# Linear attention and SwiGLU on one core: loads of a batch held until the features of the batch ahead are turned, q loaded first, first batch in fewer loads, first two weight blocks alone

## The chip, the core and the metric

The kernel runs on one core of a Trainium2 chip. A core has five engines with an instruction stream each: TensorE (PE; its weight loads are shown apart as PEld), VectorE (DVE), ScalarE (ACT), GpSimd (POOL) and SyncE (SP). Sixteen DMA engines move data between device memory (HBM) and on-chip memory (SBUF); here POOL's queue issues the loads that cast float32 to bfloat16, and SP's queue issues the first batch's float32 loads, the transposing DMAs and the output stores. TensorE writes to PSUM, eight banks of 128 x 512 float32. The metric is the device time of one execution in microseconds (us); less is better.

## The reference

q, k and v have 8 batches, 8 heads, 576 positions and 64 elements a head. The attention is linear: a feature map of 128 elements for q and for k, and no softmax. Its output, 4608 tokens of 512, goes through a SwiGLU block with 1536 hidden elements.

```python
def _attn_ref(q, k, v):
    theta = np.pi / 2.0 * pos / S
    def phi(x, c, s):
        r = np.maximum(x, 0.0)
        return np.concatenate([r * c, r * s], axis=-1)
    q_p, k_p = phi(q, cos_w, sin_w), phi(k, cos_w, sin_w)
    kv = np.einsum('bhsf,bhsd->bhfd', k_p, v)
    z = np.sum(k_p, axis=2)
    num = np.einsum('bhsf,bhfd->bhsd', q_p, kv)
    den = np.einsum('bhsf,bhf->bhs', q_p, z)[..., None] + 1e-06
    return num / den

def _moe_ref(x, w_gate, w_val, w_out):
    g = x @ w_gate
    silu = g * (1.0 / (1.0 + np.exp(-g)))
    return silu * (x @ w_val) @ w_out
```

## The kernel before

**Tiles and groups.** Positions are cut into 9 slices of 64 per batch, 72 in all. Two slices make a tile of 128 tokens (36 tiles, t), four tiles make a group of 512 tokens (9 groups, tg). Batch b begins at slice 9b, so a tile can span two batches: tile 13 holds the last slice of batch 2 and the first of batch 3. Tiles 9 to 12 are of batch 2 alone.

**The feed-forward of a group.** `ffn_fc` (line 492) computes one block fc of 128 hidden elements: four products with w_gate and four with w_val (L480), a Silu on ScalarE (L488) and a product on DVE (L490). There are 12 blocks. Then `ffn_out` (L499) does the output product of each of the four tiles, 12 products each (L507), copies it from PSUM (L514) and stores it with two DMAs on SP (L517).

**Attention of a batch, from batch 2 on.** Everything is written once per batch into slots of the feed-forward's schedule:

- `load(b, nm)` (L94) loads q, k or v of a batch on POOL's queue into one of three buffers per tensor (`raw`, bufs=3).
- `phi_q(b, g)` (L224), for each of four pairs of heads g: relu on ScalarE (L213), product with the table of cosines and sines on DVE (L230), into `r_q`.
- `relu_k` and `vmul` (L217, L233): relu of k on ScalarE (on DVE for batch 1), v times the table on DVE (L234), into `v2s` (two buffers).
- `qturn_dma(b, e)` (L250): the features of half of the heads are turned by a transposing DMA on SP's queue, from `r_q` to `phit[b][:, e]` (L253; `phit` has two buffers).
- `kv_mm(b, j)` (L267), 36 products each (L276), and `kv_out2` (L294), which copies the sums out.
- `a_tile2(t)` (L369): 8 products of the turned features with the sums (L380; 16 where the tile spans two batches), then the normalisation on DVE (L391, L393, L398). The first four wait for half e=0 of the features, the others for e=1.
- `x_turn(t)` (L447): the normalised tile is turned, by a transposing DMA on SP (L465) or, with fast, by TensorE and a copy on ScalarE (L462, L463).

Batches 0 and 1 take other paths. Batch 0's v, k and part of q are loaded as float32 on SP's queue (`load_first`, L114) into memory that w_out and the hidden activations use later. Its k is cast and clipped by `relu_first_k` (L221), and `kv_first` (L304) makes the sums in two halves.

**Slots.** `plan` maps a slot number to functions; `at(s, f)` adds one and `slot(s)` calls them, in the order in which they were added. Group tg has the slots 16 tg to 16 tg + 15: one after each of the 12 blocks, then one after each of the four output tiles. In the loop over b (L655), s0 = 16 (b - 1) is the first slot of the group ahead of the one in which the batch's middle tiles are computed, and p0 = s0 - 16. For b of 3 and more, before the change, the eight steps of k, v and q stand in slots p0 + 3 to p0 + 10 (one later for b = 3), the turning DMAs in p0 + 12 and p0 + 13, the kv products in s0 + 1 and s0 + 2. For b = 2 they stand in s0 to s0 + 3, s0 + 2, and s0 + 4 and s0 + 5.

**What sets the order.** The schedule is written by hand (`manual_schedule`): each engine runs its instructions in the order in which the program emits them, and waits only for data and for buffers. POOL has hardly anything but DMA issues after the start, so the slot in which a load is emitted fixes only its place in POOL's queue. At the start, POOL waits with the tiny copy into `hold` (L541) for v's second pair of heads; then it issues the weights in pairs of 128 columns (`load_w`, L199: w_gate, then w_val), with the loads of batch 0's remaining q and of batch 1 between them, then w_out and batch 2. PSUM banks are handed out by `take`, the one longest unused first.

**Lines the change touches.** 118 to 125 (first loads), 199 (`load_w`), 540 to 556 (POOL's first queue), 580 and 581 (first relus), 655 to 690 (slots of the batches, slots of the tiles, loads of batch 3).

Of the kernel before, what the change touches and what calls it, by code (L numbers as in the profile page):

```python
# [10 lines left out]
BF16 = mybir.dt.bfloat16  # L11
# [6 lines left out]
def kernel(  # L18
# [10 lines left out]
    nc = tc.nc  # L29
    B, H, S, D = q.shape  # L30
    P = 128
    G = H // 2
# [13 lines left out]
    consts = ctx.enter_context(tc.tile_pool(name="consts", bufs=1))  # L46
# [38 lines left out]
    def source(b, nm):  # L85
        t = {"q": q, "k": k, "v": v}[nm]
        return t[b].rearrange("(g e) (p c) d -> (e p) g (c d)", e=2, c=NC)

    def raw_of(b, nm):
        if (b, nm) not in raws:  # L90
            raws[b, nm] = raw.tile([P, G, NC, D], BF16, name=f"raw_{nm}")
        return raws[b, nm]

    def load(b, nm, parts=1):  # L94
        t, sv, n = raw_of(b, nm), source(b, nm), G // parts
        for i in range(parts):
            sl = slice(i * n, (i + 1) * n)
            nc.gpsimd.dma_start(out=t[:, sl].rearrange("p g c d -> p g (c d)"), in_=sv[:, sl])  # L98

    def load_slots(b, nm, lo, hi):  # L100
        nc.gpsimd.dma_start(out=raw_of(b, nm)[:, :, lo:hi].rearrange("p g c d -> p g (c d)"),
                            in_=source(b, nm)[:, :, lo * D:hi * D])
# [11 lines left out]
    def load_first(nm, gs, lo=0, hi=NC):  # L114
        nc.sync.dma_start(out=first[nm][:, gs, lo:hi].rearrange("p g c d -> p g (c d)"),
                          in_=source(0, nm)[:, gs, lo * D:hi * D])

    for gs in (slice(0, 1), slice(1, 2), slice(2, 4)):
        load_first("v", gs)
    load_first("k", slice(0, 1))  # L120
    load_first("k", slice(1, 2))
    load_first("q", slice(0, G), 0, 2)
    load_first("k", slice(2, 3))
    load_first("k", slice(3, 4))
    load_first("q", slice(0, G), 2, 4)
    NW = 8
    pos = consts.tile([P, NC], FP32)
# [17 lines left out]
    def idle_products(n, cols=P):  # L145
# [37 lines left out]
        out=tab.rearrange("p c e d -> p (c e) d"),  # L183
        in_=csk.rearrange("p c e -> p (c e)").to_broadcast([P, NC * 2, D]),
# [11 lines left out]
    wv_r = moe_w_val.rearrange("(c p) f -> p c f", p=P)  # L196
    wo_r = moe_w_out.rearrange("(c p) f -> p c f", p=P)

    def load_w(i):  # L199
        fs = slice(2 * i * P, (2 * i + 2) * P)  # L200
        nc.gpsimd.dma_start(out=wg_sb[:, :, fs], in_=wg_r[:, :, fs])  # L201
        nc.gpsimd.dma_start(out=wv_sb[:, :, fs], in_=wv_r[:, :, fs])

    def load_wo(i):
        cs = slice(4 * i, 4 * i + 4)
        nc.gpsimd.dma_start(out=wo_sb[:, cs], in_=wo_r[:, cs])
# [4 lines left out]
    def relu_op(eng, out, in_):  # L211
        if eng == "act":
            nc.scalar.activation(out=out, in_=in_, func=AF.Relu)  # L213
        else:
            nc.vector.tensor_single_scalar(out=out, in_=in_, scalar=0.0, op=ALU.max)

    def relu_k(b, lo, hi, eng):  # L217
        o = raw_of(b, "k")[:, lo:hi]
        relu_op(eng, o, o)

    def relu_first_k(g, eng, lo=0, hi=NC):  # L221
        relu_op(eng, raw_of(0, "k")[:, g, lo:hi], first["k"][:, g, lo:hi])

    def phi_q(b, g):  # L224

        if g == 0:
            st[b, "q"] = rel.tile([P, G, NC, 2, D], BF16, name="r_q")
        o = raws[b, "q"][:, g]
        relu_op("act", o, o)
        nc.vector.tensor_tensor(out=st[b, "q"][:, g], in0=o.unsqueeze(2).to_broadcast([P, NC, 2, D]),  # L230
                                in1=tab, op=ALU.mult)

    def vmul(b, g):  # L233
        nc.vector.tensor_tensor(  # L234
            out=v2s[b % 2][:, g, :, :, 0:D],
            in0=(first if b == 0 and g == 0 else {"v": raw_of(b, "v")})["v"][:, g].unsqueeze(2).to_broadcast([P, NC, 2, D]),
            in1=tab, op=ALU.mult,
        )
# [9 lines left out]
    phit = {}  # L248

    def qturn_dma(b, e):  # L250
        if e == 0:
            phit[b] = phip.tile([P, 2, G, NC, SH], BF16, name="phit")
        nc.sync.dma_start_transpose(  # L253
            out=phit[b][:, e].rearrange("p g c s -> p (g c) s"),
            in_=st[b, "q"][e * SH:(e + 1) * SH].rearrange("p g c w d -> p (g c w d)"),
        )
# [10 lines left out]
    def kv_mm(b, j):  # L267
        if j == 0:
            st[b, "kvps"] = take(2, ("kv", b))
        ps = st[b, "kvps"]  # L270
        for c in range(NC):
            for i in range(2):
                for e in range(2):
                    es = slice(e * SH, (e + 1) * SH)
                    g = 2 * j + i
                    nc.tensor.matmul(  # L276
                        out=ps[i * D:(i + 1) * D, e, j * 2 * D1:(j + 1) * 2 * D1],
                        lhsT=raws[b, "k"][es, g, c],
                        rhs=v2s[b % 2][es, g, c, :, 0:D1],
                        start=(c == 0), stop=(c == NC - 1),  # L280
                    )
# [12 lines left out]
    def kv_out2(b):  # L294

        ps = st[b, "kvps"][:, :, 0:4 * J * D1 // 2].rearrange("p e (j w x) -> p e j w x", j=J, w=2)
        for w, eng in enumerate((nc.scalar.copy, nc.vector.tensor_copy)):
            for i in range(2):
                eng(out=kv2s[b % 2][w * D:(w + 1) * D, :, :, i], in_=ps[i * D:(i + 1) * D, :, :, w])

    def kv_free(b):
        give_back(("kv", b))
# [26 lines left out]
    def cast_q(c, eng):  # L329
        o = qf[:, c % 2].rearrange("p j i d -> p (j i) d")  # L330
        (nc.scalar.copy if eng == "act" else nc.vector.tensor_copy)(out=o, in_=first["q"][:, :, c])
# [206 lines left out]
    for g in range(G):  # L538
        vmul(0, g)
    hold = consts.tile([P, 1], FP32)  # L540
    nc.gpsimd.tensor_copy(out=hold, in_=first["v"][:, 1, 0, 0:1])  # L541
    load_w(0)
    load_slots(0, "q", CUT[0], NC)
    for i in range(1, 4):
        load_w(i)
    load(1, "k")
    load_w(4)
    load_w(5)
    load(1, "v", 2)
    load_slots(1, "q", 0, CUT[1])  # L550
    load_wo(0)
    load_wo(1)
    load_slots(1, "q", CUT[1], NC)
    load_wo(2)
    for nm in ("k", "v", "q"):
        load(2, nm)

    OUT = GH // 2
    SLOTS = FC + OUT
    plan = {}  # L560

    def at(s, *fns):
        plan.setdefault(s, []).extend(fns)

    def slot(s):
        for f in plan.pop(s, ()):
            f()

    def a_(t, j):
        return lambda: (a_half(t, j), x_norm(t) if j else None)  # L570

    def turn(t, fast=False):
        return lambda: x_turn(t, fast)
# [4 lines left out]


    relu_first_k(0, "act")  # L580
    relu_first_k(1, "act")
    cast_q(0, "dve")
    cast_q(1, "dve")
    kv_first(0)
# [65 lines left out]
    for i, (piece, t) in enumerate(steps0):  # L650
        ffn_out(t, 4 * piece, 4 * piece + 4)
        slot(divmod(i, 4))


    for b in range(2, B):  # L655
        s0 = SLOTS * (b - 1)
        keng = "dve" if b == 2 else "act"
        steps = [lambda b=b, g=g: (relu_k(b, g, g + 1, keng), vmul(b, g)) for g in range(G)]
        steps += [lambda b=b, g=g: phi_q(b, g) for g in range(G)]
        if b == 2:  # L660
            steps = steps[G:] + steps[:G]
            fs, tq, tk = [s0 + i // 2 for i in range(8)], (s0 + 2, s0 + 2), (s0 + 4, s0 + 5)
        else:
            p0 = s0 - SLOTS
            fs = [p0 + 3 + i + (b == 3) for i in range(8)]
            tq, tk = (p0 + 12, p0 + 13), (s0 + 1, s0 + 2)
            if b > 3:
                for s, nm in ((p0 - 2, "k"), (p0, "v"), (p0 + 2, "q")):
                    at(s, lambda b=b, nm=nm: load(b, nm))
        for s, f in zip(fs, steps):  # L670
            at(s, f)
        for e in range(2):
            at(tq[e], lambda b=b, e=e: qturn_dma(b, e))
        for j in range(J):
            at(tk[j], lambda b=b, j=j: kv_mm(b, j))
        at(tk[-1], lambda b=b: kv_out2(b))
        at(tk[-1] + 1, lambda b=b: kv_free(b))
    for t in range(2 * OUT, NTG * OUT):
        tg, i = divmod(t, OUT)
        s = SLOTS * (tg - 1) + (4 if tg > 2 or i == 0 else 5) + 2 * i  # L680
        if t == 2 * OUT:
            at(s, a_(t, 0))
            at(s + 1, a_(t, 1), turn(t))
        elif tg == 2:
            at((10, 11, 12)[i - 1] + SLOTS, lambda t=t: a_tile2(t))
            at((12, 13, 14)[i - 1] + SLOTS, turn(t, True))
        else:
            at(s, lambda t=t: a_tile2(t), turn(t))
    for nm in ("k", "v", "q"):
        load(3, nm)  # L690
    for tg in range(1, NTG):
        s0 = SLOTS * tg
        for fc in range(FC):
# [39 lines left out]
```

## Time and profile before

| | us |
|---|---|
| runs | 352.4, 348.9, 351.09 (median 351.09) |
| the profiled execution | 351.02 |
| its span | 348.9 |
| TensorE busy | 324.5 (93%) |
| DVE busy | 179.3 (51%) |
| ScalarE busy | 134.9 (39%) |
| POOL busy | 31.6 (9%) |

The span runs from the first to the last instruction of the program; 2.1 us of the execution lie around it. Mean granted TensorE clock over the span: 0.974 of full speed.

How to read the lines. In the 40 slices a digit is the busy share of a slice in tenths, 9 is 90% or more. The timeline gives the start, the duration, the engine, the line, the operation and how many were merged, and in brackets how long the engine was idle just before and what ended that. In the chain of waits a row is the start, the length and what the chain went through; a DMA's row lasts from its issue to its landing. In groups of instructions the bar is followed by the busy time and the mean ns of one, then the idle time before them. A DMA issue is told with the median time from issue to landing. DMA-issuing instructions of SP are not counted as busy; the time shown for them is how long they hold SP's queue.

### The profile page before, as it was taken

The numbers are of one execution on the slowest core, as the hardware profiler recorded it, in microseconds if no ns is written. First come the engines' busy times: TensorE is split into PE (matmuls) and PEld (weight loads), VectorE is DVE, ScalarE is ACT, GpSimd is POOL, SyncE is SP. The second block draws the span as 40 slices with busy tenths as digits, with TensorE's granted clock in tenths as the row PEclk, the third lists the DMA queues.
The fourth block names the chain that finished last, engine by engine and source line by source line (L and its number), as shares of the span: only waits on it lengthen the run. The fifth ranks groups of instructions, "written<-read, shape, count | busy, mean of one in ns | idle before, by whom it ended". The sixth has DMA issues, their size and how long they took to land.

```text
span 348.9 us, 6209 instructions
## 1 busy us (share of the span) xinstructions
PE 324.5 (93%) x2484; PEld 165.6 (47%) x2484; DVE 179.3 (51%) x365; ACT 134.9 (39%) x253; POOL 31.6 (9%) x49
## 2 busy tenths in 40 slices
PE   8889999992079999999999999999999999999995
PEld 4577855440034444445445444544444444444443
DVE  6674766980072497149625952694256225603320
ACT  6544365972013464146414632562242123213321
POOL 7545320020000100020000000000000000000000
PEclk9999999998569999999999999999999999999999
DMA  7999999999926895789395129413931230231004
GB/s 226 238 200 201 203 208 233 233 160 134 134 38 114 147 190 75 128 138 195 62 152 107 31 49 154 86 30 72 152 72 39 57 81 15 41 81 45 2 22 98
DMA packets 69852, 40.51 MB, mean 116 GB/s; under 512 B 43584, under 2 KB 64320, under 8 KB 69824
## 3 DMA queue, kind: packets, MB, share of 16 engines
q1 hardware_dynamic: 49584, 22.55, 35.8%
q0 software_dynamic: 20080, 17.44, 32.4%
q8 instruction: 19, 0.31, 0.4%
q10 hardware_dynamic: 160, 0.13, 0.1%
q14 instruction: 9, 0.07, 0.1%
HBM read 37.75 MB, written 9.44 MB: 135 GB/s over the span
## 4 chain that ended last, share of the span: by engine, by line
PE 83%; DMA 14%; POOL 1%; issue 0%; ACT 0%; ACTq 0%; SPq 0%; DVE 0%; DVEq 0%
PE banks L480 50%; PE banks L507 26%; DMA phit<-r_q 6%; DMA wv_sb<-in_moe_w_val_dram 4%; DMA wg_sb<-in_moe_w_gate_dram 3%; PE banks L276 3%; PE banks L380 2%; DMA wo_sb<-in_v_dram 1%; PE banks L415 1%; PE banks L526 0%; PE banks L462 0%; PE banks L262 0%; POOL hold L541 0%; POOL wg_sb L201 0%; ACT ob L529 0%
## 5 line engine op out<-in xcount | busy, mean ns | idle before, releaser
L488 ACT ACTIVATE sg<-banks 128x512 bf16<-128x512 f32 (+2 forms) x124 | 67.2, 542 | 130.1 <-PE banks L480 122.1
L480 PE MATMUL banks<-xT,wv_sb 128*128 128x512 bf16 (+2 forms) x496 | 114.6, 354 | 1.4 <-DMA wv_sb<-in_moe_w_val_dram 1.4
L480 PE MATMUL banks<-xT,wg_sb 128*128 128x512 bf16 (+2 forms) x496 | 114.8, 354 | 0.1
L490 DVE TENSOR_TENSOR ht<-sg,banks 128x512 bf16<-128x512 bf16 (+2 forms) x124 | 76.4, 617 | 60.4 <-PE banks L480 51.3
L507 PE MATMUL banks<-wo_sb,ht 128*128 128x512 bf16 x420 | 94.3, 379 | 0.0
L480 PEld LDWEIGHTS <-wv_sb 128*128 128x128 bf16 x496 | 47.6, 98 | 48.6 <-DMA wv_sb<-in_moe_w_val_dram 1.8
L480 PEld LDWEIGHTS <-wg_sb 128*128 128x128 bf16 x496 | 44.8, 98 | 39.7 <-issue 0.6
L507 PEld LDWEIGHTS <-ht 128*128 128x128 bf16 x420 | 40.5, 98 | 46.7 <-issue 0.4
L514 DVE COPY ob<-banks 128x512 f32<-128x512 f32 x17 | 11.7, 691 | 64.7 <-PE banks L507 60.2
L514 ACT COPY ob<-banks 128x512 f32<-128x512 f32 x18 | 10.5, 586 | 58.4 <-PE banks L507 58.4
L380 PE MATMUL banks<-kv,phit 128*128 128x65 bf16 (+1 forms) x240 | 12.0, 198 | 16.6 <-DMA phit<-r_q 16.6
L230 DVE TENSOR_TENSOR r_q<-raw_q,tab 128x1152 bf16<-128x1152 bf16 x24 | 17.9, 751 | 18.7 <-DMA phit<-r_q 18.7
L234 DVE TENSOR_TENSOR v<-raw_v,tab 128x1152 bf16<-128x1152 bf16 x31 | 23.1, 753 | 2.2 <-ACT raw_v L537 2.2
L380 PEld LDWEIGHTS <-phit 128*128 128x128 bf16 (+1 forms) x240 | 10.7, 103 | 24.1 <-DMA phit<-r_q 17.3
L398 DVE TENSOR_TENSOR x<-banks,rec 128x512 bf16<-128x512 f32 (+1 forms) x32 | 21.5, 674 | 1.1
L213 ACT ACTIVATE raw_k<-raw_k 128x576 bf16<-128x576 bf16 x24 | 16.0, 675 | 0.0
L213 ACT ACTIVATE raw_q<-raw_q 128x576 bf16<-128x576 bf16 x24 | 16.0, 674 | 0.0
L98 POOL DMA_DIRECT2D raw_k<-in_k_dram x7 | 5.2, 742 | 98.3 <-issue 63.3
L276 PEld LDWEIGHTS <-raw_k 64*64 64x64 bf16 x504 | 7.8, 106 | 5.6 <-issue 4.7
L148 PE MATMUL banks<-zeros 128*128 128x64 bf16 (+1 forms) x64 | 9.4, 311 | 1.0 <-DVE zeros L143 1.0
L276 PE MATMUL banks<-v,raw_k 64*64 64x130 bf16 x504 | 10.2, 220 | 0.0
L463 ACT COPY xT<-banks 128x512 bf16<-128x512 bf16 x10 | 5.9, 588 | 3.9 <-PE banks L462 3.9
(81 smaller groups left out, 129.4 us busy)
## 6 DMA issues: line engine op xcount, KB each, us to landing
out_dram<-ob SPq DMA_DIRECT2D x70, 128.0 KB, 2.4
raw_k<-in_k_dram POOLq DMA_DIRECT2D x7, 576.0 KB, 16.5
raw_v<-in_v_dram POOLq DMA_DIRECT2D x6, 576.0 KB, 18.6
raw_q<-in_q_dram POOLq DMA_DIRECT2D x6, 576.0 KB, 20.8
wg_sb<-in_moe_w_gate_dram POOLq DMA_DIRECT2D x6, 256.0 KB, 12.2
wv_sb<-in_moe_w_val_dram POOLq DMA_DIRECT2D x6, 256.0 KB, 12.2
wo_sb<-in_moe_w_out_dram POOLq DMA_DIRECT2D x3, 512.0 KB, 13.1
ht<-in_k_dram SPq DMA_DIRECT2D x4, 288.0 KB, 6.6
```

Of the source, the lines that this page charges most:

```text
L148: nc.tensor.matmul(out=ps, lhsT=zeros, rhs=zeros[:, 0:cols].unsqueeze(1).to_broadcast([P, 4, cols]), start=True, stop=True)
L213: nc.scalar.activation(out=out, in_=in_, func=AF.Relu)
L230: nc.vector.tensor_tensor(out=st[b, "q"][:, g], in0=o.unsqueeze(2).to_broadcast([P, NC, 2, D]), in1=tab, op=ALU.mult)
L234: nc.vector.tensor_tensor(out=v2s[b % 2][:, g, :, :, 0:D], in0=(first if b == 0 and g == 0 else {"v": raw_of(b, "v")})["v"][:, g].unsqueez ...
L276: nc.tensor.matmul(out=ps[i * D:(i + 1) * D, e, j * 2 * D1:(j + 1) * 2 * D1], lhsT=raws[b, "k"][es, g, c], rhs=v2s[b % 2][es, g, c, :, 0:D ...
L380: nc.tensor.matmul(out=ps[ms, e, g * D1:(g + 1) * D1], lhsT=phit[b][:, e, g, c:c + n].rearrange("p c s -> p (c s)"), rhs=kv2s[b % 2][:, e, ...
L398: nc.vector.tensor_tensor(out=xv[:, :, ys], in0=num[:, :, ys, 0:D], in1=rv[:, :, ys].to_broadcast([P, 2, ys.stop - ys.start, D]), op=ALU.mult)
L480: nc.tensor.matmul(out=o, lhsT=w[:, kc, fs], rhs=xT[tg][:, ts, kc], start=(kc == 0), stop=(kc == KC - 1))
L488: nc.scalar.activation(out=sg[:, 0:n], in_=ps[0], func=AF.Silu)
L490: nc.vector.tensor_tensor(out=hts[tg % 2][:, fc, r:r + n], in0=sg[:, 0:n], in1=ps[1], op=ALU.mult)
L507: nc.tensor.matmul(out=o_ps[t], lhsT=hts[tg % 2][:, fc, r:r + P], rhs=wo_sb[:, fc], start=(fc == 0), stop=(fc == FC - 1))
L514: (nc.scalar.copy if t % 2 == 0 else nc.vector.tensor_copy)(out=ob, in_=ps)
```

## The change

Six edits:

1. The first batch: v in two loads of two pairs of heads, k in two, with q's two parts between and behind them; six DMAs on SP in place of nine.
2. `load_w(i, n)` loads n blocks of 128 columns from block i; the first two blocks are loaded alone, the other ten in pairs as before.
3. `relu_first_k(1)` runs on DVE in place of ScalarE.
4. Batch 2 is loaded in the order q, k, v (before: k, v, q).
5. The loads of batches 3 to 7 are emitted by `load_behind(b)`, in slot p0 + 3 for batch 3 and p0 + 1 for the others, q first. A POOL copy of two elements of `phit[b - 1]`, one of each half, stands ahead of them in POOL's queue.
6. Slots for b of 3 and more: the q steps come ahead of the k and v steps, all from p0 + 11 on; turning DMAs in p0 + 15 and p0 + 16; kv products in s0 + 4 and s0 + 5 as for batch 2. The tiles of group 3 and later move one slot back (4 + 2i becomes 5 + 2i). The rule for group 2 is written differently, and its tiles keep their slots.

```diff
-    for gs in (slice(0, 1), slice(1, 2), slice(2, 4)):
-        load_first("v", gs)
-    load_first("k", slice(0, 1))
-    load_first("k", slice(1, 2))
+    load_first("v", slice(0, 2))
+    load_first("v", slice(2, 4))
+    load_first("k", slice(0, 2))
     load_first("q", slice(0, G), 0, 2)
-    load_first("k", slice(2, 3))
-    load_first("k", slice(3, 4))
+    load_first("k", slice(2, 4))
     load_first("q", slice(0, G), 2, 4)
...
-    def load_w(i):
-        fs = slice(2 * i * P, (2 * i + 2) * P)
+    def load_w(i, n=2):
+
+        fs = slice(i * P, (i + n) * P)
...
-    load_w(0)
+    load_w(0, 1)
+    load_w(1, 1)
     load_slots(0, "q", CUT[0], NC)
-    for i in range(1, 4):
+    for i in (2, 4, 6):
         load_w(i)
     load(1, "k")
-    load_w(4)
-    load_w(5)
+    load_w(8)
+    load_w(10)
...
-    for nm in ("k", "v", "q"):
+    for nm in ("q", "k", "v"):
         load(2, nm)
...
-    relu_first_k(1, "act")
+    relu_first_k(1, "dve")
...
+    def load_behind(b):
+
+        nc.gpsimd.tensor_copy(out=hold2, in_=phit[b - 1][0:1, :, 0, 0, 0])
+        for nm in ("q", "k", "v"):
+            load(b, nm)
...
-        steps = [lambda b=b, g=g: (relu_k(b, g, g + 1, keng), vmul(b, g)) for g in range(G)]
-        steps += [lambda b=b, g=g: phi_q(b, g) for g in range(G)]
+        steps = [lambda b=b, g=g: phi_q(b, g) for g in range(G)]
+        steps += [lambda b=b, g=g: (relu_k(b, g, g + 1, keng), vmul(b, g)) for g in range(G)]
         if b == 2:
-            steps = steps[G:] + steps[:G]
-            fs, tq, tk = [s0 + i // 2 for i in range(8)], (s0 + 2, s0 + 2), (s0 + 4, s0 + 5)
+            fs, tq = [s0 + i // 2 for i in range(8)], (s0 + 2, s0 + 2)
         else:
             p0 = s0 - SLOTS
-            fs = [p0 + 3 + i + (b == 3) for i in range(8)]
-            tq, tk = (p0 + 12, p0 + 13), (s0 + 1, s0 + 2)
-            if b > 3:
-                for s, nm in ((p0 - 2, "k"), (p0, "v"), (p0 + 2, "q")):
-                    at(s, lambda b=b, nm=nm: load(b, nm))
+            fs, tq = [p0 + 11 + i for i in range(8)], (p0 + 15, p0 + 16)
+            at(p0 + 3 if b == 3 else p0 + 1, lambda b=b: load_behind(b))
+        tk = (s0 + 4, s0 + 5)
...
-        s = SLOTS * (tg - 1) + (4 if tg > 2 or i == 0 else 5) + 2 * i
+        s = SLOTS * (tg - 1) + (5 if tg > 2 else 4) + 2 * i
...
-    for nm in ("k", "v", "q"):
-        load(3, nm)
```

More of the change, by code (lines that the diff above doesn't have):

```diff
@@ L540 @@
     hold = consts.tile([P, 1], FP32)
+    hold2 = consts.tile([1, 2], BF16)
     nc.gpsimd.tensor_copy(out=hold, in_=first["v"][:, 1, 0, 0:1])
-    load_w(0)
+    load_w(0, 1)
+    load_w(1, 1)
     load_slots(0, "q", CUT[0], NC)
-    for i in range(1, 4):
+    for i in (2, 4, 6):
         load_w(i)
     load(1, "k")
-    load_w(4)
-    load_w(5)
+    load_w(8)
+    load_w(10)
     load(1, "v", 2)
```

## The prediction

> **What bounds the kernel now.** I read the page's 40 slices first, then the chain of waits, then the timeline around the gap. One slice is 348.9 / 40 = 8.72 us.
>
> ```profile
> PE   8889999992079999999999999999999999999995
> PEclk9999999998569999999999999999999999999999
> DMA  7999999999926895789395129413931230231004
> ```
>
> TensorE is full from slice 3 on except around slices 9 to 11 (a gap near 87 us), where its granted clock (PEclk, tenths) falls to a half; and the DMA engines are full from the start right up to that hole. After it they are seldom full. The chain of waits says what TensorE waited for, and shows undisturbed stretches of the same work further on:
>
> ```profile
> 69.41 1.73 PE banks L480 x8
> ...
> 76.21 21.52 DMA phit<-r_q
> ...
> 97.78 0.40 PE banks L380 x4
> 98.18 3.41 PE banks L480 x8
> ...
> 101.99 2.59 PE banks L507 x12
> ...
> 104.80 0.26 PE banks L380 x8
> ...
> 113.28 3.45 PE banks L480 x16
> ...
> 127.14 0.38 PE banks L380 x16
> ...
> 136.77 10.36 PE banks L507 x48
> ...
> 170.39 10.36 PE banks L507 x48
> ```
>
> Timeline, TensorE, with the idle time before each row in brackets:
>
> ```profile
> 79.72 1.03 PE L480 MATMUL banks<-xT,wv_sb 128*128 128x512 bf16 x4
> 88.55 0.40 PE L380 MATMUL banks<-kv,phit 128*128 128x65 bf16 x4 [7.80 <-DMA phit<-r_q]
> 97.78 0.40 PE L380 MATMUL banks<-kv,phit 128*128 128x65 bf16 x4 [8.83 <-DMA phit<-r_q]
> ```
>
> This is tile 9, the first that reads the turned q features of batch 2: it waits 7.80 us for the first half and 8.83 us for the second, 16.63 us in all. Why those two transposes were late (POOL's and SP's queues; then all twelve transposes: shortest, median and longest ns on SP's queue, and us to landing):
>
> ```profile
> 53.70 0.74 POOL L98 DMA_DIRECT2D raw_q<-in_q_dram  x1 [5.35 <-PE banks L262]
> 72.33 0.74 POOL L98 DMA_DIRECT2D raw_k<-in_k_dram  x1 [17.89 <-issue]
> 120.41 0.74 POOL L98 DMA_DIRECT2D raw_k<-in_k_dram  x1 [45.44 <-issue]
> 65.60 27.46 SPq L253 DMA_TRANSPOSE phit<-r_q  x2
> 105.23 1.80 SPq L517 DMA_DIRECT2D out_dram<-ob  x2
> 107.13 3.60 SPq L253 DMA_TRANSPOSE phit<-r_q  x1
> L253 SPq DMA_TRANSPOSE phit<-r_q x12: 3474/3604/16857, 65.6 to 248.0; - x12
> DMA to landing us min/median/max: 5.9/6.1/22.9
> ```
>
> The pair issued at 65.60 held SP's queue for 27.46 us; an undisturbed one takes 3.60 us there and lands after 6.1. Beside them POOL's loads were in flight: batch 4's (q issued at 53.70) and, from 72.33, batch 5's. POOL runs ahead of the order in which its loads are written: only a buffer that is still read stops it (three per tensor). So batches 3 to 5 are loaded before batch 2's features are turned. The landings of single loads, in us from their issue (DMA issues in a narrow stretch each, in this order: q at 53.70, k at 72.33, k at 120.41, v at 121.14):
>
> ```profile
> raw_q<-in_q_dram POOLq DMA_DIRECT2D x1, 576.0 KB, 25.2
> raw_k<-in_k_dram POOLq DMA_DIRECT2D x1, 576.0 KB, 16.8
> raw_k<-in_k_dram POOLq DMA_DIRECT2D x1, 576.0 KB, 6.5
> raw_v<-in_v_dram POOLq DMA_DIRECT2D x1, 576.0 KB, 8.7
> ```
>
> A load behind others needs 25.2 us; the first of a trio on an empty queue 6.5, the next 2.9 more (121.14 + 8.7 - 120.41 - 6.5).
>
> **The change, part by part.** *Held loads (the gain).* The tiny POOL copy in load_behind reads both halves of batch b-1's turned features, so no load of batch 3 or later is in flight while batch 2's transposes run. Batch 2's own three loads keep their place behind the last of the w_out loads, q now first, and nothing is put ahead of them. At 65.6 us only output stores are left beside the transposes, as at 107.13, where one took 3.60 and landed after 6.1. So I take: second one issued at 65.60 + 3.60 = 69.2, landed at 75.3. TensorE wants it at 79.72 + 1.73 / 2 = 80.6, so the wait goes with 5.3 us to spare. What that is worth: from 80.6 TensorE had a tile (0.26), a block (1.73) and a tile (0.26) to do before the first output products, which would then start at 80.6 + 2.25 = 82.83; they started at 101.99. That is 19.16 us: 16.63 of waiting, and 2.5 because the clock came back slowly (the eight products of L480 took 3.41 for 1.73). Bounds: nothing (if the transposes were slow by themselves) to 19.16; I take 19.16, by the rows of the other ten transposes.
>
> *What is late next.* Group 2's first block moves from 113.28 to 113.28 - 19.16 = 94.1. Batch 3's loads now start when POOL's copy has run, 75.3 + 0.85 (the row of the other POOL hold, below) = 76.15, q first: landed at 76.15 + 6.5 = 82.65, k at 85.5, v near 88.5. Its relu is due in slot 27, at 80.6 + 0.26 + 1.73 = 82.6. So q comes about when it is wanted. If it is later, ScalarE waits there, with four q relus, three copies of turned tiles and two output copies (taken as long as a tile's) to do before group 2 needs them. The page's rows, busy us and mean ns of one behind the bar, and the POOL copy:
>
> ```profile
> L213 ACT ACTIVATE raw_q<-raw_q 128x576 bf16<-128x576 bf16 x24 | 16.0, 674 | 0.0
> L463 ACT COPY xT<-banks 128x512 bf16<-128x512 bf16 x10 | 5.9, 588 | 3.9 <-PE banks L462 3.9
> L514 DVE COPY ob<-banks 128x512 f32<-128x512 f32 x17 | 11.7, 691 | 64.7 <-PE banks L507 60.2
> L230 DVE TENSOR_TENSOR r_q<-raw_q,tab 128x1152 bf16<-128x1152 bf16 x24 | 17.9, 751 | 18.7 <-DMA phit<-r_q 18.7
> 4.39 0.85 POOL L541 COPY hold<-wo_sb 128x1 f32<-128x1 f32 x1 [1.87 <-DMA wo_sb<-in_v_dram]
> ```
>
> That is 4 x 0.67 + 5 x 0.59 = 5.6 us; q may land as late as 94.1 - 5.6 = 88.5 before TensorE feels it. Then batch 3's transposes: moved from slots 28 and 29 to 31 and 32, on SP behind the stores of all four output tiles instead of one. The last tile's copy (0.69) and two stores (1.80 at 105.23) are done 2.5 us into group 2 (96.6); two transposes of 3.6 and a landing of 6.1 give 96.6 + 3.6 + 6.1 = 106.3. Their first reader, the tile that spans batches 2 and 3 (127.14 above), moves one block back, to 127.14 - 19.16 + 1.73 = 109.7: 3.4 us to spare. From there the loop repeats each group of 33.6 us (136.77 to 170.39): transposes landed 12.2 us in, q landed 0.85 + 6.5 later at 19.6, its relu due after the twelfth block at 136.77 - 113.28 = 23.5. It fits with 3.9 us, and the readers of batches 4 to 7 come later in their groups (blocks 9 and 11). k and v, 2.9 and 5.8 us behind q, are due four output tiles later, 23.5 + 10.36.
>
> *Moved work.* The eight feature steps of a batch are the same instructions in later slots, four of them now beside output products, where DVE and ScalarE have less to do; tiles move one slot and kv products three, so that in slot 5 the kv copies, a tile's normalisation and the block's product fall on DVE together. Batch 2 already runs its kv products in slots 4 and 5, and TensorE has no idle time at the second of them (a row without brackets):
>
> ```profile
> 71.06 0.72 PE L276 MATMUL banks<-v,raw_k 64*64 64x130 bf16 x36
> ```
>
> I take 0, bounds 0 to 0.4 us a batch, 2 us in all. The xT transposes of the last tile come one block (1.73) later and have the output products as cover (10.36). Five POOL copies cost nothing: POOL waits 17.89 and 45.44 us in the rows above, and behind each copy stand only the loads it is meant to hold.
>
> *The first 31 us.* Timeline rows:
>
> ```profile
> 11.10 0.45 DVE L215 TENSOR_SCALAR raw_k<-ht 128x576 bf16<-128x576 f32 x1
> 11.84 0.33 DVE L215 TENSOR_SCALAR raw_k<-ht 128x320 bf16<-128x320 f32 x1 [0.28 <-DMA ht<-in_k_dram]
> 18.42 0.74 POOL L202 DMA_DIRECT2D wv_sb<-in_moe_w_val_dram  x1 [0.58 <-DMA wg_sb<-in_moe_w_gate_dram]
> 19.73 0.74 POOL L201 DMA_DIRECT2D wg_sb<-in_moe_w_gate_dram  x1 [0.57 <-DMA wv_sb<-in_moe_w_val_dram]
> 19.48 0.23 PEld L480 LDWEIGHTS <-wv_sb 128*128 128x128 bf16 x4 [1.08 <-DMA wv_sb<-in_moe_w_val_dram]
> 30.99 0.33 PEld L480 LDWEIGHTS <-wv_sb 128*128 128x128 bf16 x4 [0.72 <-DMA wv_sb<-in_moe_w_val_dram]
> ```
>
> SP issues six loads instead of nine; the bytes and their order are nearly the same, and the queue is full, so landings hardly move. k's groups 2 and 3 now land together, at about 11.8, so DVE does the relu of 0.45 after that too: +0.4 us, less some 0.3 if the earlier issue helps; group 1's relu goes from ScalarE to DVE, behind the v products, for about the same. This is covered: TensorE waits 1.08 us for weights at 19.48. Without that cover it would cost the 0.4. Splitting the first weight pair gives two more loads with rows half as long. A 256 KB load takes 1.31 us (18.42 to 19.73: each issue waits for a landing), a 576 KB load 2.9, so time goes by bytes and I take +0.2 us; the upper bound is that a half takes as long as a whole, 2 x 1.31 = 2.6 us, which the wait at 30.99 would pass on; the lower is -0.5.
>
> A page speaks against the split: the Trainium skill, "DMA: Bandwidth & Descriptors", section Specifications, puts the shortest transfer at line rate at 512 B, with a read-modify-write below, and the split rows are 256 B in bf16. By it the halves would take about double, which is the upper bound just worked out; no transfer of POOL with such rows is in this trace.
>
> **Sum.** The profiled execution took 351.02 us (span 348.9), beside a median of 351.09: 351.02 - 19.16 + 0.2 = 332.1 us.
>
> **The rivals.**
>
> (a) *The prologue pays for the halves*: 332.1 - 0.2 + 2.6 = 334.5 us. For: the DMA engines are full until 96 us, so every landing would shift. Against: 256 KB and 576 KB loads cost the same per byte.
>
> (b) *The wait moves to batch 3's loads, once*: q needs 16.8 us (what k at 72.33 needed) instead of 6.5 and lands at 93.0, 4.5 us later than ScalarE can bear, plus about 1 for the clock: 337.6 us (the 1 is an estimate, less than the 2.5 after the longer wait). For: q is due at the moment it lands. Against: nothing large is in flight beside it.
>
> (c) *Slower: the hold closes a loop.* Load, features, two transposes and POOL's copy of each batch now follow one another: L + 4 x 0.75 + 0.67 + 3.6 + 6.1 + 0.85 = L + 14.2, once per group of 33.6 us. It decides from L = 19.4 us. With the 25.2 of the load at 53.70, each of five batches costs 5.8 us: 332.1 + 29 = 361 us. Against: that load stood behind four others; one that starts on an empty queue took 6.5.
>
> The Trainium skill ("DMA: Bandwidth & Descriptors", Rules for kernel authors) says to issue a DMA early and wait for it late, which is against holding loads back; this trace shows the price of early loads, 16.63 us of TensorE's time.
>
> (d) *The change doesn't do what it says*: the transposes are as slow without loads beside them, 351.0 + 0.2 = 351.2 us. Against: ten others at 3.5 to 3.6 us.
>
> **How the numbers follow.** The forecast 0.82; (a) 0.06; (b) 0.06; (c) 0.03; (d) 0.03. The range takes the forecast with its bounds (-0.5 in the prologue, about +2 for the moved work, and the spread of the runs, 348.9 to 352.4, 1.7 either way), (a) and half of (b): 329.8 to 337.5. About 1% is what a measurement of this kernel can tell from no change. Faster by over 1%: 0.82 + 0.06 + 0.06 = 0.94; within 1%: (d), 0.03; slower: (c), 0.03.
>
> **What would show it.** Right: both transposes of batch 2 at about 3.6 us on SP's queue, no TensorE wait for phit near 81 us, POOL's three loads of batch 3 issued near 76 in the order q, k, v, the granted clock at 1.00 from 31 us to the end, and one trio of loads in each group of 33.6 us. Wrong: TensorE or ScalarE waiting for raw_q in slots 27 to 30 or at block 11 of a group; a wait for phit at the first tile of a batch; the weight waits near 19 and 31 us grown by over 1 us.

## The result, and the profile after

The change takes 331.76 us (median of four, 331.19 to 332.38) beside 350.29 of the kernel before (median of four, 348.9 to 352.4): a ratio of 0.947, 95% interval 0.941 to 0.952. The forecast was 332.1 with a range of 329.8 to 337.5. The profiled execution took 331.19 us, its span is 329.4, and its mean granted TensorE clock 1.00 where it was 0.974. Ratios here and below leave out executions more than 1.5% above the fastest of their kernel (in the last series 9 of 17 of the kernel before, so ratios compare only within a series), and medians leave out two that are far out, 674.97 us of the change in after_again and 1180.34 of start_only.

The 40 slices of the page after the change (8.24 us each):

```profile
PE   8889999999999999999999999999999999999995
PEclk9999999999999999999999999999999999999999
DMA  7999998298858797969597959795932411341014
```

The hole in TensorE's row and the dip of its clock are gone. In the DMA row, counted from slice 0, the block of nines that reached to slice 10 now ends with slice 5, and slice 7 reads 2. The 9 of slice 8 (65.9 to 74.1 us) is batch 2's two transposes: there only SP's queue has packets (1.06 MB). The loads behind it are spread over the groups.

The chain of waits after the change (start, length, what it went through):

```profile
59.09 8.63 PE banks L479 x40
...
80.03 0.26 PE banks L379 x8
...
82.28 2.59 PE banks L506 x12
...
93.56 8.63 PE banks L479 x40
...
109.15 0.38 PE banks L379 x16
...
117.06 10.36 PE banks L506 x48
```

Line numbers are one lower than before: L479 is a block's product, L379 a tile, L506 an output product. For the start of group 1 the chain before has this row:

```profile
59.80 8.63 PE banks L480 x40
```

These rows divide the gain by stage. Group 1 starts at 59.09 for 59.80: 0.71 us came before it. Group 2 starts at 93.56 for 113.28: 19.72 in all, so the gap gave 19.72 - 0.71 = 19.01 us. The output products of group 2 start 117.06 - 93.56 = 23.50 us into it, before 136.77 - 113.28 = 23.49. The last output products begin at 315.19 for 334.91, again 19.72 earlier: behind group 2's start TensorE won and lost nothing. The span fell by 19.5.

SP's and POOL's queues after the change, then all twelve transposes of features, and the landings of two loads of q (issued at 76.28 and at 108.39):

```profile
64.91 8.78 SPq L252 DMA_TRANSPOSE phit<-r_q  x2
95.52 8.20 SPq L252 DMA_TRANSPOSE phit<-r_q  x2
75.77 0.17 POOL L657 COPY hold<-phit 1x2 bf16<-1x2 bf16 x1 [38.90 <-DMA phit<-r_q]
76.28 0.74 POOL L98 DMA_DIRECT2D raw_q<-in_q_dram  x1 [0.34 <-issue]
77.02 0.75 POOL L98 DMA_DIRECT2D raw_k<-in_k_dram  x1
...
107.88 0.18 POOL L657 COPY hold<-phit 1x2 bf16<-1x2 bf16 x1 [29.37 <-DMA phit<-r_q]
108.39 0.74 POOL L98 DMA_DIRECT2D raw_q<-in_q_dram  x1 [0.34 <-PE banks L479]
L252 SPq DMA_TRANSPOSE phit<-r_q x12: 3443/4052/5176, 64.9 to 234.3; - x12
DMA to landing us min/median/max: 6.5/7.1/9.0
raw_q<-in_q_dram POOLq DMA_DIRECT2D x1, 576.0 KB, 5.8
raw_q<-in_q_dram POOLq DMA_DIRECT2D x1, 576.0 KB, 7.9
```

Batch 2's pair holds SP's queue for 8.78 us where it held it for 27.46. The copy runs as soon as the pair has landed (its idle time of 38.90 ends with the DMA), and the trio of loads goes out behind it, in the order written. Where a DMA row is `x2`, its length is that of both on the queue.

### The profile page after: what moved, and what is told of

Same layout as the page of the kernel before. It is cut to its first block, busy times and chain, and to the rows that moved or that the text cites. A ratio compares the mean times of both kernels' runs of the same rounds, so it can differ in the third digit from the quotient of the medians.

```text
span 329.4 us, 6225 instructions
## 1 busy us (share of the span) xinstructions
PE 322.2 (98%) x2484; PEld 165.1 (50%) x2484; DVE 182.5 (55%) x366; ACT 134.3 (41%) x252; POOL 33.3 (10%) x56
## 4 chain that ended last, share of the span: by engine, by line
PE 89%; DMA 8%; POOL 1%; ACT 0%; ACTq 0%; issue 0%
PE banks L479 54%; PE banks L506 28%; DMA wv_sb<-in_moe_w_val_dram 4%; DMA wg_sb<-in_moe_w_gate_dram 3%; PE banks L275 3%; PE banks L379 2%; DMA wo_sb<-in_v_dram 1%; PE banks L414 1%; PE banks L525 0%; POOL wg_sb L200 0%; PE banks L461 0%; POOL wv_sb L201 0%; PE banks L261 0%; ACT ob L528 0%; POOL raw_q L101 0%
## 5 line engine op out<-in xcount | busy, mean ns | idle before, releaser
L479 PE MATMUL banks<-xT,wv_sb 128*128 128x512 bf16 (+2 forms) x496 | 113.7, 352 | 1.0 <-DMA wv_sb<-in_moe_w_val_dram 1.0
L479 PE MATMUL banks<-xT,wg_sb 128*128 128x512 bf16 (+2 forms) x496 | 113.9, 352 | 0.3 <-DMA wg_sb<-in_moe_w_gate_dram 0.3
L506 PE MATMUL banks<-wo_sb,ht 128*128 128x512 bf16 x420 | 94.3, 379 | 0.0
L479 PEld LDWEIGHTS <-wv_sb 128*128 128x128 bf16 x496 | 47.4, 98 | 47.7 <-DMA wv_sb<-in_moe_w_val_dram 1.5
L479 PEld LDWEIGHTS <-wg_sb 128*128 128x128 bf16 x496 | 45.5, 98 | 41.5 <-DMA wg_sb<-in_moe_w_gate_dram 0.4
L506 PEld LDWEIGHTS <-ht 128*128 128x128 bf16 x420 | 40.0, 98 | 45.4 <-issue 0.4
L513 DVE COPY ob<-banks 128x512 f32<-128x512 f32 x17 | 11.7, 691 | 28.6 <-PE banks L506 27.6
L397 DVE TENSOR_TENSOR x<-banks,rec 128x512 bf16<-128x512 f32 (+1 forms) x32 | 21.5, 674 | 1.1
L657 POOL COPY hold<-phit 1x2 bf16<-1x2 bf16 x5 | 0.9, 175 | 159.7 <-DMA phit<-r_q 159.7
L379 PEld LDWEIGHTS <-phit 128*128 128x128 bf16 (+1 forms) x240 | 9.9, 100 | 6.0 <-issue 1.3
L379 PE MATMUL banks<-kv,phit 128*128 128x65 bf16 (+1 forms) x240 | 11.5, 195 | 0.0
L298 DVE CAST kv<-banks 64x260 bf16<-64x260 f32 x12 | 5.1, 428 | 4.3 <-ACT kv L298 4.2
```

The source lines that it names most:

```text
L379: nc.tensor.matmul(out=ps[ms, e, g * D1:(g + 1) * D1], lhsT=phit[b][:, e, g, c:c + n].rearrange("p c s -> p (c s)"), rhs=kv2s[b % 2][:, e, ...
L397: nc.vector.tensor_tensor(out=xv[:, :, ys], in0=num[:, :, ys, 0:D], in1=rv[:, :, ys].to_broadcast([P, 2, ys.stop - ys.start, D]), op=ALU.mult)
L479: nc.tensor.matmul(out=o, lhsT=w[:, kc, fs], rhs=xT[tg][:, ts, kc], start=(kc == 0), stop=(kc == KC - 1))
L506: nc.tensor.matmul(out=o_ps[t], lhsT=hts[tg % 2][:, fc, r:r + P], rhs=wo_sb[:, fc], start=(fc == 0), stop=(fc == FC - 1))
L513: (nc.scalar.copy if t % 2 == 0 else nc.vector.tensor_copy)(out=ob, in_=ps)
```

## The experiments

Twelve runs, one of them the change itself again. Each is the change with the edit shown, unless said otherwise; the change stands at 331.2 to 332.4 us in the runs above.

**The hold alone taken away.** Order and slots of the change stay.

```diff
-        nc.gpsimd.tensor_copy(out=hold2, in_=phit[b - 1][0:1, :, 0, 0, 0])
```

> The changed kernel without the five POOL copies, so that POOL's loads run ahead again; everything else as changed. My theory (loads beside the transposes of batch 2 make them late): the wait of TensorE for phit at tile 9 comes back, 15 to 18 us plus 2 to 3 us at a slow clock, and the time is about 331.5 + 19 = 350 us (347 to 353). Rival (the new slots or the first batch's loads made the kernel faster): no wait for phit, and 331 to 333 us.

343.87 us (343.52 to 344.48), below the 347 to 353 that were expected; ratio to the kernel before 0.981 (0.975 to 0.987). TensorE's waits and timeline, then POOL's and SP's queues, then the landing of v:

```profile
PE banks L379 <- DMA phit<-r_q: 10.0, 2, 8.4
88.44 0.40 PE L379 MATMUL banks<-kv,phit 128*128 128x65 bf16 x4 [8.36 <-DMA phit<-r_q]
90.44 0.40 PE L379 MATMUL banks<-kv,phit 128*128 128x65 bf16 x4 [1.60 <-DMA phit<-r_q]
65.24 0.74 POOL L98 DMA_DIRECT2D raw_q<-in_q_dram  x1 [9.80 <-PE banks L479]
...
72.40 0.75 POOL L98 DMA_DIRECT2D raw_v<-in_v_dram  x1
64.96 23.01 SPq L252 DMA_TRANSPOSE phit<-r_q  x2
raw_v<-in_v_dram POOLq DMA_DIRECT2D x1, 576.0 KB, 16.0
```

The wait for the turned features is back, at the same tile, so it was the hold that took it away. But it is 10.0 us and not the 16.63 of the kernel before. With q first, batch 5's q goes out at 65.24, when batch 2's q is read, and no longer waits behind k, which found its buffer free at 72.33. So the last load lands at 72.40 + 16.0 = 88.4 us; before it was this one, issued third at 74.22:

```profile
74.22 0.75 POOL L98 DMA_DIRECT2D raw_q<-in_q_dram  x1
raw_q<-in_q_dram POOLq DMA_DIRECT2D x1, 576.0 KB, 22.2
```

It landed at 96.4. In both kernels the second transpose comes in 1 to 2 us after the last of these loads. The hold is worth 343.87 - 331.76 = 12.1 us beside the other edits; these alone are worth 350.91 - 343.87 = 7.0. The shorter wait (6.6 us) accounts for most of the 7.0, and the rows above put it down to the order of the loads; the order was not run alone.

**The hold with the slots of before.** Steps, turning DMAs, kv products and tiles of batch 3 and later go back to their old slots; the loads stay behind the hold.

```diff
-        steps = [lambda b=b, g=g: phi_q(b, g) for g in range(G)]
-        steps += [lambda b=b, g=g: (relu_k(b, g, g + 1, keng), vmul(b, g)) for g in range(G)]
+        steps = [lambda b=b, g=g: (relu_k(b, g, g + 1, keng), vmul(b, g)) for g in range(G)]
+        steps += [lambda b=b, g=g: phi_q(b, g) for g in range(G)]
...
-            fs, tq = [p0 + 11 + i for i in range(8)], (p0 + 15, p0 + 16)
+            fs = [p0 + 3 + i + (b == 3) for i in range(8)]
+            tq, tk = (p0 + 12, p0 + 13), (s0 + 1, s0 + 2)
...
-        s = SLOTS * (tg - 1) + (5 if tg > 2 else 4) + 2 * i
+        s = SLOTS * (tg - 1) + 4 + 2 * i
```

> The changed kernel with the slots of before for the feature steps, transposes, kv products and tiles, the hold kept. My theory (held loads need the later slots): batch 3's k is asked for in slot 20, near 69 us, and cannot land before 85, so ScalarE and then TensorE wait some 13 us there; each later batch asks 7 us into its group for a load that lands 11 us in, 4 us each, four times. About 360 us (345 to 370), with idle time of ScalarE ended by raw_k or raw_q loads. Rival (the hold alone is enough): 331 to 334 us.

392.16 us, one run: slower than the kernel before by 41, and worse than expected. The list of waits and the timeline:

```profile
DVE v L233 <- DMA raw_v<-in_v_dram: 57.4, 5, 18.8
...
ACT raw_k L212 <- DMA raw_k<-in_k_dram: 48.8, 5, 17.8
...
PE banks L379 <- DVE x L397: 32.5, 4, 8.4
...
85.23 0.68 ACT L212 ACTIVATE raw_k<-raw_k 128x576 bf16<-128x576 bf16 x1 [17.81 <-DMA raw_k<-in_k_dram]
88.08 0.76 DVE L233 TENSOR_TENSOR v<-raw_v,tab 128x1152 bf16<-128x1152 bf16 x1 [18.79 <-DMA raw_v<-in_v_dram]
89.29 1.86 PE L479 MATMUL banks<-xT,wg_sb 128*128 128x512 bf16 x4 [17.95 <-DVE num L425]
```

ScalarE and DVE stand at the front of their queues before loads that the hold has only just let go, with the feed-forward's own work behind them, and TensorE waits for that: once 17.95 us, and four times, 32.5 us in all, for the normalisation of a tile (L397). The expectation had counted k and forgotten v, the third of the trio, which is wanted in the same slots. So the hold and the later slots belong together: either alone loses most of the gain or more than it.

**q last behind the hold.** q lands later, and the loop of rival (c) gets longer.

```diff
-        for nm in ("q", "k", "v"):
+        for nm in ("k", "v", "q"):
```

> The changed kernel with the held loads in the order k, v, q. q then lands 5 to 6 us later, some 12 to 14 us after the first issue. My theory (the loop of load, features, transposes and copy has room until q needs 19.4 us): 331 to 333 us, the same within 0.5%, with ScalarE waiting for q at block 11 but TensorE not. Rival (q is due 3.9 us after it lands, and each us beyond that is paid by TensorE in each of five batches): 2 us x 5, 340 us or more.

342.56 us (339.81 to 345.43), ratio 0.980 (0.971 to 0.988): my theory fell, the rival held. The timeline of ScalarE, DVE and TensorE at batch 5's load of q, with one row of the chain of waits, the DMA:

```profile
159.88 0.68 ACT L212 ACTIVATE raw_q<-raw_q 128x576 bf16<-128x576 bf16 x1 [7.40 <-DMA raw_q<-in_q_dram]
160.59 0.76 DVE L229 TENSOR_TENSOR r_q<-raw_q,tab 128x1152 bf16<-128x1152 bf16 x1 [7.16 <-ACT raw_q L212]
161.70 0.69 DVE L397 TENSOR_TENSOR x<-banks,rec 128x512 bf16<-128x512 f32 x1
162.42 2.43 DMA xT<-x
164.99 1.02 PE L479 MATMUL banks<-xT,wg_sb 128*128 128x512 bf16 x4 [1.73 <-DMA xT<-x]
```

Read downwards, each row releases the next. In the slot of block 11 the first q step is emitted ahead of the group's last tile. DVE runs in order, so the tile's normalisation (L397) stands behind the first q product; the turning of that tile waits for it, and so does the next group's first block. q landed at 159.86, the turned tile at 164.85: q has to be there 5.0 us before the next group begins. By the profile of the change q is issued 108.39 - 93.56 = 14.8 us into a group of 33.6, so a load of q may take 33.6 - 14.8 - 5.0 = 13.8 us, not 19.4. The size of the wait agrees: the group of these rows began at 129.66 in the chain, so q landed 30.2 us into it, 1.6 us later than 33.6 - 5.0 = 28.6, and TensorE waited 1.73.

**q much later.** k and v are loaded three times ahead of q (the extra loads write the same data again), to see what a stall costs.

```diff
-        for nm in ("q", "k", "v"):
+        for nm in ("k", "v") * 3 + ("q",):
```

> The changed kernel with k and v of a held batch each loaded three times (the same data into the same buffers) and q behind them, so that q lands some 27 to 30 us after the hold ends. My theory (rival c of the prediction: the loop L + 14.2 must fit a group of 33.6 us): 8 to 11 us of TensorE's time in each of five batches, 370 to 388 us, with TensorE idle. Rival (ScalarE and PSUM banks have enough room that late loads don't reach TensorE): below 340 us.

410.73 us, one run: (410.73 - 331.8) / 5 = 15.8 us a batch, above the 8 to 11 expected. The list of TensorE's waits (total, times, longest) names the same place:

```profile
PE banks L479 <- DMA xT<-x: 53.3, 4, 14.3
```

**The tile ahead of the q steps, q still last.** If the account above is right, the wait goes when the first two steps of batches 3 and later are added to their slots after the tiles.

```diff
+    later = []
...
+        if b > 2:
+            later += list(zip(fs, steps))[:2]
+            fs, steps = fs[2:], steps[2:]
...
+    for s, f in later:
+        at(s, f)
```

> q_last, and the first two feature steps of each batch from 3 on are added to their slots behind the tiles, so that in block 11's slot the group's last tile is normalised ahead of the first q product on DVE. New theory (q last costs because that tile stands behind a product that waits for q, its turning DMA leaves late, and the next group's first block waits for it): 331 to 333 us, with ScalarE still waiting for q but TensorE not. Rival (ScalarE's wait for q reaches TensorE by itself, through output copies and banks): 338 us or more.

331.45 us (330.90 to 331.76), ratio 0.953 (0.945 to 0.961). The tile's product is now ahead of q's, and although ScalarE waits up to 9.1 us for q, the list of waits has no TensorE wait for xT any more (timeline of DVE, list of waits):

```profile
151.97 0.69 DVE L397 TENSOR_TENSOR x<-banks,rec 128x512 bf16<-128x512 f32 x1
159.05 0.76 DVE L229 TENSOR_TENSOR r_q<-raw_q,tab 128x1152 bf16<-128x1152 bf16 x1 [6.39 <-ACT raw_q L212]
...
ACT raw_q L212 <- DMA raw_q<-in_q_dram: 39.1, 5, 9.1
```

**The same with q much later.** Tile first, and `("k", "v") * 3 + ("q",)`.

> q_late with the same order of slots as the run before this one in the list. q lands 26 to 29 us after the hold ends. If the loop of the prediction (L + 14.2 against 33.6 us) binds once the tile is out of the way: 7 to 10 us in each of five batches, 365 to 382 us, with no wait of TensorE for xT. If ScalarE's copies hold TensorE as well: 390 us or more.

397.97 us, one run, as the second expectation had it: TensorE's waits for xT are gone, but in four groups it now waits for ScalarE, whose output copies stand behind its wait for q and hold the PSUM banks that TensorE needs (TensorE's waits; beside this row one wait of 14.1 us for a tile's normalisation):

```profile
PE banks L479 <- ACT ob L513: 37.0, 4, 10.8
```

**The tile ahead of the q steps in the change itself**, q first as it was.

> The changed kernel with those two feature steps behind the tiles and nothing else changed. Theory: in the change q lands in time, so the order in the slot is worth nothing: 331 to 332.5 us, the same within 0.2%. Rival (a tenth of the waits is still there in every batch): 0.5 to 1 us faster.

331.20 us (330.63 to 331.42), ratio 0.952 (0.947 to 0.957). It isn't measurably faster than the change, whose list of waits has no wait of TensorE behind the start; by tile_first_q_last it leaves more room for a late load.

**The first 31 us.** Three edits, one at a time, run beside the change itself once more.

> The changed kernel once more, beside the next three on the same chip. 331 to 332.5 us; group 1's first block at 59.1 us, the first weight load issued at 4.45 us, POOL's first hold 0.18 us long.

331.45 us (330.82 to 332.75), ratio 0.946 (0.943 to 0.949). Its profile is of the execution of 674.97 us and says nothing of the start, so for that the rows of the change's first profile are used.

```diff
-    load_first("v", slice(0, 2))
-    load_first("v", slice(2, 4))
+    for gs in (slice(0, 1), slice(1, 2), slice(2, 4)):
+        load_first("v", gs)
```

> The changed kernel with v's first two pairs of heads in two loads again, as before the change. In the kernel before, POOL's hold copy ran from 4.39 to 5.24 and ended with DVE's first v product (3.75 to 5.20); after the change it ran ahead of that product and took 0.18. My theory (the copy stands still while DVE's product runs, and the start of all weight loads with it): the copy takes about 0.85 again, the first weight load is issued near 5.2, group 1 starts 0.6 to 0.8 us later, about 0.7 us more in all. Rival (fewer, larger loads land sooner by themselves): the copy stays at 0.18 and group 1 moves by less than 0.2 us.

332.99 us (331.66 to 334.56), ratio 0.950 (0.947 to 0.954). Group 1 starts 1.9 us later. Chain, then timeline of DVE and POOL, then v's last load, of this kernel:

```profile
1.67 6.49 DMA wo_sb<-in_v_dram
...
60.95 8.63 PE banks L479 x40
3.75 1.45 DVE L233 TENSOR_TENSOR v<-wo_sb,tab 128x1152 bf16<-128x1152 f32 x1
4.37 0.87 POOL L541 COPY hold<-wo_sb 128x1 f32<-128x1 f32 x1 [1.85 <-DMA wo_sb<-in_v_dram]
wo_sb<-in_v_dram SPq DMA_DIRECT2D x1, 576.0 KB, 6.5
```

The same rows of the change:

```profile
4.32 0.18 POOL L541 COPY hold<-wo_sb 128x1 f32<-128x1 f32 x1 [1.80 <-DMA wo_sb<-in_v_dram]
4.37 1.36 DVE L233 TENSOR_TENSOR v<-wo_sb,tab 128x1152 bf16<-128x1152 f32 x1 [0.35 <-DMA wo_sb<-in_v_dram]
4.45 0.89 POOL L200 DMA_DIRECT2D wg_sb<-in_moe_w_gate_dram  x1
wo_sb<-in_v_dram SPq DMA_DIRECT2D x1, 576.0 KB, 4.5
```

Where v comes in one load of two pairs, POOL's copy starts ahead of DVE's product, takes 0.18 us and not 0.87, and the first weights go out at 4.45; where the first pair comes alone, the product starts first and the copy ends only when it does (4.37 + 0.87 = 5.24, 3.75 + 1.45 = 5.20), with the first weights behind it. So the copy does as expected, and v's last load takes longer, 6.5 us for 4.5. But the chain of this kernel goes through that load (landed at 1.67 + 6.49 = 8.16) and batch 0's attention to group 1, and through neither the copy nor a weight load. The 1.9 us go with v's later landing, which neither expectation had at this size; a share of the copy in them is not shown.

```diff
-    nc.gpsimd.tensor_copy(out=hold, in_=first["v"][:, 1, 0, 0:1])
```

> The changed kernel without POOL's first hold, so that the weight loads are issued from about 2.6 us on, beside the first loads of v and k. If the end of the start goes with the first weight issue, as the theory for v_apart has it, group 1 starts up to 1.8 us sooner (57.3 to 58.5) and the kernel takes about 330 us. Rival (the DMA engines are full there, and v and k come later): group 1 at 59 to 61 us, no gain or a loss up to 2 us.

332.0 us (331.17 to 332.31), ratio 0.947 (0.944 to 0.949), group 1 no earlier:

```profile
60.06 8.63 PE banks L479 x40
```

The first weights go out 2.0 us sooner, at 2.46, and it brings nothing; in both kernels the DMA row reads 9 in slices 1 to 5.

```diff
-    load_w(0, 1)
-    load_w(1, 1)
+    load_w(0)
```

> The changed kernel with the first two weight blocks in one pair of loads again. By my prediction the halves cost 0.2 us, so this is the same within 0.3 us. If rows of 256 B took as long as rows of 512 B, the pair would save up to 2.6 us: 329 us, with group 1 at 56.5 to 58 us.

331.19 us (330.55 to 331.52), ratio 0.944 (0.942 to 0.947), group 1 here:

```profile
58.97 8.63 PE banks L479 x40
```

So the two halves cost 0.1 us at group 1's start and 0.3 in the medians (331.45 against 331.19), less than the spread of either.

**Edits 1 to 3 alone**, on the kernel before.

> The kernel before with edits 1 to 3 alone (first batch in six loads, first two weight blocks alone, one relu on DVE). Theory: the start gains what it gained in the change, 0.7 us, and the wait for phit at tile 9 stays (16 to 17 us): 350.3 us beside 351.0 of before, TensorE's granted clock down to 0.5 after it. Rival (the first batch's loads are a cause of the late transposes): the wait shrinks by several us.

349.52 us (344.41 to 351.4), ratio 0.998 (0.991 to 1.004): no difference that can be measured. Its chain and timeline (line numbers two lower than before), with the gap still there:

```profile
61.18 8.63 PE banks L478 x40
...
91.09 0.40 PE L378 MATMUL banks<-kv,phit 128*128 128x65 bf16 x4 [8.84 <-DMA phit<-r_q]
```

This execution took 344.41, the shortest of that kernel: here only the second transpose was waited for. The wait is smaller by several us, as the rival had it, but the medians of the two kernels don't differ, so edits 1 to 3 are not shown to shorten it. That the wait varies suggests why the kernel before runs between 345.0 and 352.4 us while the change stays between 330.8 and 332.8; no profile of a short execution of the kernel before was taken. Group 1 starts at 61.18 here, 1.38 us later than in the profile of the kernel before, though POOL's copy takes 0.18 us here too.

## Why the prediction was right

**The gain (19.16 forecast, 19.01 measured): right, and for the reason given.** The second transpose was put at 75.3 us and landed at about 75.7 (the copy that waits for it starts at 75.77); the output products of group 1 were put at 82.83 - 0.71 for the earlier start and began at 82.28. Taking the hold out brings the wait back, at the same tile and released by the same DMA. What the prediction didn't see is that the 19 us are not the hold's alone: beside the other edits the hold is worth 12.1 us, and the rest comes with those edits, by the rows of no_hold with the order of the loads. Rival (d), that the transposes are slow by themselves, is out. That 332.1 lies 0.3 us from the median is in part luck: the sum is built for the profiled execution, which took 331.19, and the 0.9 us between the two are about what the start was off.

**The start (+0.2 forecast, -0.71 between the two profiles): sign and cause are open.** The step costed edits 1 to 3 by bytes and took landings as they were. Two things that it left out stand in the rows: POOL's first copy takes 0.18 us where it took 0.85 beside DVE's first product, and v's last load landed 1.7 us sooner (at 5.8 for 7.4). That they make up the 0.71 is not shown: weights that went out 2.0 us sooner brought nothing in no_first_hold, and in the profile of start_only the same three edits go with a group 1 that starts 1.38 us later than before, so single profiles differ by more than the amount to be explained. By start_only all of this is too small to be measured as an edit of its own. The upper bound, a half load as long as a whole one, is out by first_pair, and rival (a) with it. The Trainium skill ("DMA: Bandwidth & Descriptors", section Specifications) puts the shortest transfer at line rate at 512 B, from which the prediction took it that rows of 256 B double the time; the 0.1 to 0.3 us over four half loads don't agree with that. The rows read from HBM are of 128 float32, 512 B, so reads below that length were not tried.

**Moved work (0 forecast): right**, 23.50 against 23.49 us in group 2.

**What is late next: the times right, the room too large.** The loads of batch 3 were put at 76.15 and went out at 76.28; q was put at 82.65 and landed at 76.28 + 5.8 = 82.1, so rival (b) didn't come; ScalarE waited 0.30 us for it and TensorE not at all. Batch 3's transposes were put at 106.3 and landed at 107.7, with 1.4 us to spare where 3.4 were forecast; batch 4's q landed at 108.39 + 7.9 = 116.3, or 22.7 us into the group, 0.8 ahead of its relu and not 3.9. Two terms were mis-sized. The load of q took 7.9 us for 6.5. The pair of transposes was taken at 3.60 each and 6.1 to landing; here the median holds the queue for 4.05 us, the longest for 5.18, and lands after 7.1, at most 9.0. The rows for 3.60 and 6.1 were of transposes that went out singly: in the kernel before the ten later ones are 5.5 to 5.8 us apart. In the change both of a pair go out back to back; the first holds the queue for 3.4 to 3.7 us, the second for 4.4 to 5.2. That this is the cause is likely and not shown: no run of the change has the two set apart.

**Rival (c), the loop: its deciding point wrong.** The mechanism is there, but it decides from about 13.8 us and not from 19.4. The step asked how late q's transposes may be and what ScalarE has left to do (q "may land as late as 88.5"). It left out DVE, where the last tile of a group stands behind the first q product. The bound that binds first was found only by q_last, in which the load of q took up to 13.9 us (issued at 146.00, landed at 159.86) and the time rose by 11. Since the loads of the change take 5.8 to 7.9 us, the forecast didn't depend on it; the chance of 0.03 was too low for a margin of 6 us.

## What to carry to other kernels

A prefetch that fills the DMA engines costs the small transfer that an engine will wait for next, and a tiny copy in the issuing queue that reads that transfer's result is enough to hold the prefetch back; but the work that uses the held loads has to move as far as the loads did. Where a change adds a wait, look at what stands behind it in every in-order queue that takes part, not in the one engine that waits, and put work that the critical engine needs next ahead of it in the slot. Write loads in the order in which their buffers come free: one whose buffer is still read keeps back all behind it in the queue.

## What was not expected of the hardware

- Of two transposes beside queued loads the second landed only 0.7 to 2.0 us behind the last of those loads, however early the first was issued: at 97.7 us where that load landed at 96.4 (kernel before), at 90.4 where it landed at 88.4 (no_hold), at 91.0 where it landed at 90.3 (start_only). The first wasn't bound so: it landed at 88.5, 88.4 and, in start_only, at 79.7. With no such load in flight the second was there at 75.7.
- POOL's copy of 128 elements takes 0.85 to 0.87 us while DVE multiplies two operands in SBUF, and 0.18 where it starts 0.05 us ahead of the product. The Trainium skill ("SBUF — State Buffer", section Who interferes with whom) has it that a DVE instruction with two SBUF inputs contends with a GpSimd instruction that reads SBUF, and that the port they share is an exclusive lock; these rows agree.
